# Cross-covariance attention with a highway layer: the loads' order, the start, and the place of one copy

## The chip, the cores and the metric

One core of a Trainium2 chip. The metric is the device time of one execution in microseconds (us); several executions of a kernel are timed and their median is compared. The engines are TensorE (PE, with its weight loads as PEld), VectorE (DVE), ScalarE (ACT), GpSimd (POOL) and SyncE (SP).

## What is computed

Inputs are float32: q, k, v of 4 batches x 6336 rows x 256 columns, two weights of 256x256, one bias. In short:

```python
qn = q / (norm(q, axis=1) + 1e-6);  kn = k / (norm(k, axis=1) + 1e-6)
a  = softmax(kn.transpose(0, 2, 1) @ qn / tau)      # 256 x 256 per batch
x  = (v @ a).reshape(25344, 256)
H  = maximum(x @ w_h, 0);  T = sigmoid(x @ w_t + b_t)
out = T * H + (1 - T) * x
```

## The kernel before

A batch is 49 tiles of 128 rows and a rest of 64 rows. **Phase 1** of a batch (`p1_tile`, L155) reads q and k and builds S = k'q and the diagonal blocks G of k'k and q'q in two PSUM banks, tile after tile. The **chain** (`chain`, L188) turns them into `mr`, a matrix of 256x768 that holds a, a·w_h and a·w_t: norms on DVE, a square root on POOL (`nrm`, L206), softmax on ACT and DVE, then products with the weights. **Phase 2** works in 25 slots per batch, 100 in all, each of two tiles of v. A slot multiplies the transposed v of its tiles with the three parts of `mr` (`mains`, L343, into `zbank`, `h`, `x`), and the same PE stream transposes v for the slot three ahead (`transpose`, L317, into the one PSUM buffer `vtps`), which `vt_copy` (L333) copies to SBUF as `vts`: on DVE for odd slots, on ACT for even ones. `elementwise_ops` (L374) makes the output: a sigmoid `tt` and a reseeding copy on ACT, `th` and `ux` on DVE, `o` on POOL, and a store by SP every four slots.

The program is written out by hand and each engine runs its instructions in that order. Phase 1 of batch 0 stands alone at the start; phase 1 of batch b+1 is spread over the slots of batch b by `P1_END` (batch 1 in slots 0 to 17, batch 2 in 18 to 42, batch 3 in 43 to 67), and its chain follows, a piece per slot.

POOL issues all loads. They are groups of 12, 12, 12, 9 and 4 tiles of q and k (`load_qk`, six buffers each) and of 16, 16 and 17 tiles of v (`load_v`, four buffers), cast to float16 on the way: 64 KB as it lands for each tile, half of what is read. The issues take eight completion semaphores in turn (DMASW0 to 7), so each waits for the load eight before it to have landed. In the kernel before, q and k of batch 0, the weights, v's first group and the first group of batch 1 are issued ahead of the constants (`ident`, from which the other engines' start hangs), and later groups in pairs when a buffer has come free.

Of the kernel before, what the change touches and what calls it, by code (L numbers as in the profile page):

```python
# [11 lines left out]
f32 = mybir.dt.float32  # L12
# [7 lines left out]
def kernel(  # L20
# [31 lines left out]
    NQG = len(QG)  # L52
    QRING = 6
    VG = [(0, 16), (16, 16), (32, 17)]
# [14 lines left out]
    def rows(src2d):  # L69
        return src2d[0:NF, :].rearrange("(p s) c -> p s c", s=NS)  # L70
# [1 line left out]

    q_t, k_t, qr_t, kr_t, v_t = {}, {}, {}, {}, {}

    def load_qk(n):
        b, g = divmod(n, NQG)
        if b >= B:
            return
        s0, ns = QG[g]
        q_t[n] = stream_pool.tile([P, 12, C], f16, tag="q_in", bufs=QRING, name=f"q{n}")  # L80
        k_t[n] = stream_pool.tile([P, 12, C], f16, tag="k_in", bufs=QRING, name=f"k{n}")
        nc.gpsimd.dma_start(out=q_t[n][:, 0:ns, :], in_=rows(q[b])[:, s0 : s0 + ns, :])  # L82
        nc.gpsimd.dma_start(out=k_t[n][:, 0:ns, :], in_=rows(k[b])[:, s0 : s0 + ns, :])
        if g == 0:
            qr_t[b] = stream_pool.tile([P, C], f16, tag="q_rem", bufs=2, name=f"qr{b}")
            kr_t[b] = stream_pool.tile([P, C], f16, tag="k_rem", bufs=2, name=f"kr{b}")
            nc.gpsimd.dma_start(out=qr_t[b][0:REM, :], in_=q[b][NF:N, :])
            nc.gpsimd.dma_start(out=kr_t[b][0:REM, :], in_=k[b][NF:N, :])

    def load_v(m):  # L90
        b, g = divmod(m, NVG)
        if b >= B:
            return
# [42 lines left out]
    btp = hx_tile("btp")  # L136
    nc.tensor.matmul(btp[:, 0, :], ones32[0:1, :], bt_sb, start=True, stop=True)  # L137
    btb = const_pool.tile([P, 2, C], f32, tag="btb")
    for u in range(2):
        nc.scalar.copy(out=btb[:, u, :], in_=btp[:, 0, :])  # L140
    zbank = []
    for i in range(2):
        zb = psum_pool.tile([P, 2, C], f32, tag=f"z{i}", name=f"zbank{i}")
        nc.tensor.matmul(
            zb[:, :, :], zeros[:, 0:P], zeros[:, :], start=True, stop=True,
            skip_group_check=True,
        )
        nc.scalar.copy(out=zb[:, :, :], in_=btb[:, :, :])
        zbank.append(zb)
# [27 lines left out]
    def group_ended(j):  # L177

        for g, (s0, ns) in enumerate(QG):
            if j == s0 + ns:  # L180
                return g
        return None
# [222 lines left out]
    loads_due = []  # L405
    for j in range(NS + 1):
        p1_tile(0, j)
        g = group_ended(j)
        if g is not None:
            load_qk(g + QRING)  # L410
    load_v(3)

    pend = chain(0)
    vps = {}
    for idx, (pe, rest) in enumerate(pend):
        if pe is not None:
            pe()
        rest()
        if idx < LOOK:
            vt_copy(idx, transpose(idx))  # L420


    total1 = (B - 1) * (NS + 1)
    done1 = 0
    chain_q = []

    def p1_target(t):
        lo = 0
        for i, e in enumerate(P1_END):
            if t < e:  # L430
                return i * (NS + 1) + (NS + 1) * (t + 1 - lo) // (e - lo)
            lo = e
        return total1

    for t in range(NSLOT):
        b, i = divmod(t, NPAIR)
        due, loads_due = loads_due, []
# [12 lines left out]
        elementwise_ops(t, z, h, x)  # L450
        if ps is not None:
            vt_copy(t + LOOK, ps)
            bb, ii = divmod(t + LOOK, NPAIR)
            for g, (s0, ns) in enumerate(VG):
                if 2 * ii + 2 == s0 + ns or (g == NVG - 1 and ii == NPAIR - 1):
                    loads_due.append((load_v, bb * NVG + g + VRING))
        for fn, arg in due:
            fn(arg)
# [45 lines left out]
```

## Time and profile before

| | us |
|---|---|
| median of 3 runs | 371.47 (371.08 to 371.8) |
| the profiled execution: its own time | 372.11 |
| its span in the trace | 369.9 |
| PE, DVE, ACT, POOL busy | 271.1, 178.2, 164.8, 170.6 |

Busy times are sums over stages with different limits. The sum of the prediction is made against the span; 2.2 us of the execution's own time lie around it, and that execution took 0.6 us more than the median.

### The profile page before, as it was taken

How to read it: one execution, taken by the hardware profiler on the slowest of the kernel's cores; microseconds unless marked ns; L12 is line 12 of the kernel's file. 1: busy time of each engine (PE TensorE's matmuls, PEld its weight loads, DVE VectorE, ACT ScalarE, POOL GpSimd, SP SyncE). 2: the span in 40 equal slices, each digit the busy share in tenths (PEclk: the TensorE clock that was granted, in tenths of full speed). 3: DMA queues.
4: the chain of work that ended last, by engine and by line, in shares of the span. 5: the costliest groups of instructions: out<-in, count | busy, mean ns of one | idle time of the engine just before them, and what ended most of it. 6: DMA issues, size and time to landing. Idle time of an engine off the chain costs nothing.

```text
span 369.9 us, 6923 instructions
## 1 busy us (share of the span) xinstructions
PE 271.1 (73%) x2844; PEld 226.2 (61%) x2844; DVE 178.2 (48%) x333; ACT 164.8 (45%) x286; POOL 170.6 (46%) x184
## 2 busy tenths in 40 slices
PE   0001996017999998889999978999999677777781
PEld 0000896014889887768888857788888454666660
DVE  0000001024555554775656566656656776667781
ACT  1000101013545446645554657455455856666660
POOL 5213112120464477445565653445455644555563
PEclk9999999555999999899999999999999989999997
DMA  7999999999149999999899993735629123222223
GB/s 133 213 214 212 213 216 214 211 214 217 20 143 215 261 265 264 240 226 240 214 204 295 199 223 119 114 136 153 191 113 223 39 93 135 116 113 116 113 115 135
DMA packets 13377, 65.58 MB, mean 177 GB/s; under 512 B 1569, under 2 KB 3618, under 8 KB 8738
## 3 DMA queue, kind: packets, MB, share of 16 engines
q0 software_dynamic: 8992, 39.19, 54.9%
q1 hardware_dynamic: 4354, 25.96, 17.2%
q8 instruction: 22, 0.36, 0.4%
q14 instruction: 9, 0.07, 0.1%
HBM read 78.38 MB, written 25.95 MB: 282 GB/s over the span
## 4 chain that ended last, share of the span: by engine, by line
PE 46%; DVE 19%; DMA 14%; issue 9%; POOL 6%; ACT 3%; DVEq 0%; POOLq 0%; ACTq 0%
DMA q<-in_q_dram 11%; PE h L347 10%; DVE ux L392 8%; PE S L169 8%; PE vtps L324 7%; PE zbank L347 6%; PE x L347 6%; DVE vts L339 6%; PE G L172 4%; PE G L175 4%; POOL o L398 3%; DVE th L387 3%; DMA k<-in_k_dram 3%; PE ah L273 1%; POOL nrm L206 1%
## 5 line engine op out<-in xcount | busy, mean ns | idle before, releaser
L398 POOL TENSOR_TENSOR o<-th,ux 128x512 f32<-128x512 f32 x96 | 123.8, 1291 | 127.4 <-DVE ux L392 106.0
L347 PEld LDWEIGHTS <-vts 128*128 128x128 f16 x1200 | 110.5, 99 | 17.5 <-issue 6.3
L387 DVE SCALAR_TENSOR_TENSOR th<-h,tt 128x512 f32<-128x512 f32 (+1 forms) x104 | 69.3, 669 | 83.9 <-PE h L347 55.3
L377 ACT ACTIVATE tt<-zbank 128x512 f32<-128x512 f32 x100 | 59.7, 597 | 90.3 <-PE zbank L347 89.4
L169 PE MATMUL S<-q,k 128*128 128x256 f16 x392 | 87.0, 276 | 0.0
L172 PE MATMUL G<-k 128*128 128x128 f16 x392 | 76.1, 221 | 0.0
L392 DVE SCALAR_TENSOR_TENSOR ux<-tt,x 128x512 f32<-128x512 f32 (+1 forms) x104 | 67.9, 656 | 0.1
L324 PE MATMUL vtps<-ident,v 128*128 128x128 f16 (+1 forms) x400 | 40.0, 222 | 30.9 <-DVE vts L339 27.8
L347 PE MATMUL zbank<-mr,vts 128*128 128x256 f16 (+1 forms) x400 | 61.5, 276 | 0.6 <-DVE mr L286 0.6
L347 PE MATMUL x<-mr,vts 128*128 128x256 f16 (+1 forms) x400 | 61.7, 277 | 0.0
L347 PE MATMUL h<-mr,vts 128*128 128x256 f16 (+1 forms) x400 | 61.4, 276 | 0.0
L379 ACT COPY zbank<-btb 128x512 f32<-128x512 f32 x98 | 57.8, 590 | 3.1
L324 PEld LDWEIGHTS <-v 128*128 128x128 f16 (+1 forms) x400 | 27.2, 99 | 45.9 <-DVE vts L339 37.6
L175 PE MATMUL G<-q 128*128 128x128 f16 x392 | 54.2, 220 | 0.0
L169 PEld LDWEIGHTS <-k 128*128 128x128 f16 x392 | 38.7, 99 | 4.1 <-issue 0.6
L339 ACT CAST vts<-vtps 128x512 f16<-128x512 f32 x48 | 27.9, 582 | 27.3 <-PE vtps L324 27.2
L172 PEld LDWEIGHTS <-k 128*128 128x128 f16 x392 | 38.8, 99 | 0.8
L339 DVE CAST vts<-vtps 128x512 f16<-128x512 f32 x48 | 32.8, 683 | 0.0
L175 PEld LDWEIGHTS <-q 128*128 128x128 f16 x392 | 30.4, 99 | 2.4
L137 PE MATMUL btp<-bt_sb,ones 1*128 1x256 f32 x2 | 1.2, 707 | 35.7 <-DVE ones L120 35.7
L82 POOL DMA_DIRECT2D q<-in_q_dram x20 | 11.4, 568 | 29.2 <-PE G L175 19.4
L137 PEld LDWEIGHTS btp<-bt_sb,ones 1*128 1x128 f32 x2 | 0.5, 308 | 35.7 <-DVE ones L120 35.7
(55 smaller groups left out, 108.3 us busy)
## 6 DMA issues: line engine op xcount, KB each, us to landing
out_dram<-o SPq DMA_DIRECT2D x24, 1024.0 KB, 4.6
q<-in_q_dram POOLq DMA_DIRECT2D x12, 768.0 KB, 13.2
k<-in_k_dram POOLq DMA_DIRECT2D x12, 768.0 KB, 17.8
v<-in_v_dram POOLq DMA_DIRECT2D x8, 1024.0 KB, 10.6
v<-in_v_dram POOLq DMA_DIRECT2D x4, 1088.0 KB, 14.7
q<-in_q_dram POOLq DMA_DIRECT2D x4, 576.0 KB, 17.9
k<-in_k_dram POOLq DMA_DIRECT2D x4, 576.0 KB, 18.6
q<-in_q_dram POOLq DMA_DIRECT2D x4, 256.0 KB, 15.7
```

The costliest lines, as they stand in the source:

```text
L82: nc.gpsimd.dma_start(out=q_t[n][:, 0:ns, :], in_=rows(q[b])[:, s0 : s0 + ns, :])
L169: nc.tensor.matmul(S[:, c, :], kc, qq[0:nr, :], start=first and c == 0, stop=last and c == 1)
L172: nc.tensor.matmul(G[:, c, :], kc, kc, start=first and c == 0, stop=False)
L175: nc.tensor.matmul(G[:, 2 + c, :], qc, qc, start=False, stop=last and c == 1)
L324: nc.tensor.matmul(ps[:, u, c, 0 : nr[u]], vt[0 : nr[u], s + u, bass.ts(c, P)], ident[0 : nr[u], 0 : nr[u]], start=(u == 0 and c == 0), st ...
L339: cp(out=sb, in_=ps)
L347: nc.tensor.matmul(dst[0:r, u, :], sb[:, u, kt, 0:r], mr[:, kt, off : off + C], start=(not seeded and kt == 0 and (u == 0 or i == NPAIR - 1)),
L377: nc.scalar.activation(out=tt, in_=z, func=Act.Sigmoid)
L379: nc.scalar.copy(out=z, in_=btb)
L387: nc.vector.scalar_tensor_tensor(out=th[pr, us, :], in0=h[pr, us, :], scalar=0.0, in1=tt[pr, us, :], op0=AluOp.max, op1=AluOp.mult,)
L392: nc.vector.scalar_tensor_tensor(out=ux[pr, us, :], in0=tt[pr, us, :], scalar=1.0, in1=x[pr, us, :], op0=AluOp.subtract, op1=AluOp.mult,)
L398: nc.gpsimd.tensor_tensor(out=ot[pr, o0 + us.start : o0 + us.stop, :], in0=th[pr, us, :], in1=ux[pr, us, :], op=AluOp.subtract,)
```

## The change

The weights, constants and loads of the start change places; the loads of q and k are separate, sorted by the slot that needs them, and issued one per slot (three at a time at two places of the start); the groups of q and k of batches 1 to 3 run 4, 9, 12, 12, 12 tiles, and the rest of 64 rows is worked last in place of first; four tiles of batch 1's phase 1 (`HEAD`) go into the chain of batch 0, and the seeding of `zbank` from the bias (`btp`, `btb`) behind phase 1 of batch 0; the copy `vts` goes ahead of `th` and `ux`; a chain's PE piece stands behind the slot's products and its other piece behind the elementwise work.

```diff
-    QG = [(0, 12), (12, 12), (24, 12), (36, 9), (45, 4)]
+    QG = [spans(12, 12, 12, 9, 4)] + [spans(4, 9, 12, 12, 12)] * (B - 1)
+    HEAD = 4
...
-    for n in range(NQG):
-        load_qk(n)
-    wht = const_pool.tile([P, 2, 2 * C], f16, tag="wht")
...
-    load_v(0)
-    load_qk(NQG)
+    load_q(0)
+    load_k(0)
     bt_sb = const_pool.tile([1, C], f32, tag="bt")
...
     nc.vector.memset(zeros.bitcast(u16), 0)
-    load_v(1)
-    load_v(2)
+    for n in range(1, NQG):
+        load_q(n)
+        load_k(n)
+    load_qr(0)
+    load_kr(0)
+    wht = const_pool.tile([P, 2, 2 * C], f16, tag="wht")
...
+    load_q(NQG)
+    load_k(NQG)
+    load_v(0)
...
-        if j == 0:
+        if j == NS:
             kk, qq, nr = kr_t[b], qr_t[b], REM
...
-    def elementwise_ops(t, z, h, x):
+    def elementwise_ops(t, z, h, x, ps):
         nc.scalar.activation(out=tt, in_=z, func=Act.Sigmoid)
+        if ps is not None:
+            vt_copy(t + LOOK, ps)
...
+    want.sort()
+    def next_loads(k):
+        while k and want:
+            _, _, fn, arg, dep = want[0]
+            if dep is not None and dep not in ready:
+                return
+            want.pop(0)
+            fn(arg)
+            k -= 1
...
     for j in range(NS + 1):
         p1_tile(0, j)
-        if g is not None:
-            load_qk(g + QRING)
-    load_v(3)
+    ready = set(used)
+    next_loads(3)
+    btp = hx_tile("btp")
+    nc.tensor.matmul(btp[:, 0, :], ones32[0:1, :], bt_sb, start=True, stop=True)
...
+        if idx == 5:
+            next_loads(3)
+        if idx == 2:
+            while done1 < HEAD:
+                p1_tile(1, done1)
...
         mains(t, z, 2 * C, True)
         ps = transpose(t + LOOK) if t + LOOK < NSLOT else None
-        if pe_part is not None:
-            pe_part()
         mains(t, h, C, False)
         mains(t, x, 0, False)
-        if rest_part is not None:
-            rest_part()
-        elementwise_ops(t, z, h, x)
-        if ps is not None:
-            vt_copy(t + LOOK, ps)
+        if pe_part is not None:
+            pe_part()
+        elementwise_ops(t, z, h, x, ps)
+        if rest_part is not None:
+            rest_part()
+        next_loads(1)
```

POOL at the start. Before, the constant `ident` stands behind 19 loads; here the last of them (names carry the buffer's number):

```order
L96 DMA v_96<-in_v_dram 128x4096 [waits DMASW6_49]
L82 DMA q_98<-in_q_dram 128x3072 [waits DMASW7_49]
L83 DMA k_99<-in_k_dram 128x3072 [waits DMASW0_49]
L87 DMA qr_102<-in_q_dram 64x256 [waits DMASW1_49]
L88 DMA kr_103<-in_k_dram 64x256 [waits DMASW2_49]
masks.py:197 MEMSET ident_108 128x128
```

With the change the same place is reached after two loads that wait for nothing:

```order
L88 DMA q_69<-in_q_dram 128x3072
L94 DMA k_71<-in_k_dram 128x3072
masks.py:197 MEMSET ident_75 128x128
masks.py:199 ISA
masks.py:199 AFFINE_SELECT ident_75<-ident_75 128x128 [waits Pool_49]
L88 DMA q_90<-in_q_dram 128x3072
```

`ident` has moved ahead of all loads that wait for another to land. Next, POOL from the end of batch 0's phase 1, before:

```order
L82 DMA q_457<-in_q_dram 128x3072 [waits DMASW6_49,PE_49]
L83 DMA k_458<-in_k_dram 128x3072 [waits DMASW7_49]
L87 DMA qr_461<-in_q_dram 64x256 [waits DMASW0_49]
L88 DMA kr_462<-in_k_dram 64x256 [waits DMASW1_49]
L96 DMA v_465<-in_v_dram 128x4096 [waits DMASW2_49]
L206 TENSOR_TENSOR nrm_482<-n_0_468,half 128x4 [waits DVE_49]
```

and with the change, on into the first slots:

```order
L88 DMA q_425<-in_q_dram 128x3072 [waits DMASW3_49,PE_49]
L205 TENSOR_TENSOR nrm_446<-n_0_439,half 128x4 [waits DVE_49]
L206 TENSOR_TENSOR nrm_446<-nrm_446,eps 128x4 [waits Pool_49]
L94 DMA k_493<-in_k_dram 128x3072 [waits DMASW4_49]
L108 DMA v_495<-in_v_dram 128x4096 [waits DMASW5_49]
L88 DMA q_497<-in_q_dram 128x3072 [waits DMASW6_49,PE_49]
L399 TENSOR_TENSOR o_563<-th_559,ux_560 128x512 [waits DVE_49]
L94 DMA k_565<-in_k_dram 128x3072 [waits DMASW7_49]
L399 TENSOR_TENSOR o_563<-th_603,ux_604 128x512 [waits DVE_49]
L88 DMA q_608<-in_q_dram 128x3072 [waits DMASW0_49,PE_49]
```

16 loads stood between those 19 and `nrm`, 35 in all; now 20 stand ahead of it, and from slot 0 each `o` but a few is followed by one load with a wait of its own. Last, DVE in slots 0 to 2, before:

```order
L387 SCALAR_TENSOR_TENSOR th_554<-h_541,tt_551 128x512
L392 SCALAR_TENSOR_TENSOR ux_555<-tt_551,x_546 128x512
L339 CAST vts_560<-vtps_536 128x512
L387 SCALAR_TENSOR_TENSOR th_598<-h_585,tt_595 128x512
L392 SCALAR_TENSOR_TENSOR ux_599<-tt_595,x_590 128x512
```

and with the change:

```order
L338 CAST vts_556<-vtps_539 128x512
L388 SCALAR_TENSOR_TENSOR th_559<-h_544,tt_554 128x512
L393 SCALAR_TENSOR_TENSOR ux_560<-tt_554,x_549 128x512
L388 SCALAR_TENSOR_TENSOR th_603<-h_588,tt_598 128x512
L393 SCALAR_TENSOR_TENSOR ux_604<-tt_598,x_593 128x512
```

The copy stands ahead of the `th` and `ux` of its slot. PE's order within a slot (zbank, vtps, h, x, q/k tiles) is the same in both.

## Rows read from the trace of the kernel before

**Rows 1.** The page: span, granted TensorE clock and DMA share in 40 slices
```profile
span 369.9 us, 6923 instructions
...
PEclk9999999555999999899999999999999989999997
DMA  7999999999149999999899993735629123222223
```

**Rows 2.** Timeline, POOL, 0 to 37: start, us, engine line op, [idle before <-releaser]
```profile
8.77 0.54 POOL L82 DMA_DIRECT2D q<-in_q_dram  x1 [3.06 <-DMA q<-in_q_dram]
12.40 0.53 POOL L83 DMA_DIRECT2D k<-in_k_dram  x1 [3.10 <-DMA k<-in_k_dram]
...
32.94 0.52 POOL L87 DMA_DIRECT2D qr<-in_q_dram  x1 [2.19 <-DMA k<-in_k_dram]
...
35.49 1.20 POOL L96 DMA_DIRECT2D v<-in_v_dram  x2 [0.20 <-issue]
```

**Rows 3.** Timeline, PE, its first instruction
```profile
35.74 1.22 PE L137 MATMUL btp<-bt_sb,ones 1*128 1x256 f32 x2 [35.74 <-DVE ones L120]
```

**Rows 4.** Timeline, POOL, the last load ahead of batch 0's chain
```profile
77.22 0.56 POOL L96 DMA_DIRECT2D v<-in_v_dram  x1 [2.29 <-DMA q<-in_q_dram]
77.81 1.06 POOL L206 TENSOR_TENSOR nrm<-n,half 128x4 f32<-128x4 f32 x1
```

**Rows 5.** Timeline, ACT: the sigmoids of slots 0, 18, 43, 68, 75, 99
```profile
90.22 0.60 ACT L377 ACTIVATE tt<-zbank 128x512 f32<-128x512 f32 x1
...
141.29 0.60 ACT L377 ACTIVATE tt<-zbank 128x512 f32<-128x512 f32 x1
...
213.99 0.60 ACT L377 ACTIVATE tt<-zbank 128x512 f32<-128x512 f32 x1
...
286.76 0.60 ACT L377 ACTIVATE tt<-zbank 128x512 f32<-128x512 f32 x1
...
308.55 0.60 ACT L377 ACTIVATE tt<-zbank 128x512 f32<-128x512 f32 x1 [0.70 <-DVE ux L392]
...
360.37 0.60 ACT L377 ACTIVATE tt<-zbank 128x512 f32<-128x512 f32 x1 [1.02 <-PE zbank L347]
```

**Rows 6.** Timeline, PE, slots 29 and 30 (with q/k tiles)
```profile
176.04 0.60 PE L347 MATMUL zbank<-mr,vts 128*128 128x256 f16 x4
176.96 0.40 PE L324 MATMUL vtps<-ident,v 128*128 128x128 f16 x4 [0.32 <-DVE vts L339]
...
178.95 0.60 PE L347 MATMUL zbank<-mr,vts 128*128 128x256 f16 x4
...
181.37 0.49 PE L347 MATMUL zbank<-mr,vts 128*128 128x256 f16 x3
```

**Rows 7.** Timeline, PE, slots 84 and 85 (no q/k tiles left)
```profile
328.41 0.60 PE L347 MATMUL zbank<-mr,vts 128*128 128x256 f16 x4
...
329.94 0.60 PE L347 MATMUL zbank<-mr,vts 128*128 128x256 f16 x4
...
332.86 0.60 PE L347 MATMUL zbank<-mr,vts 128*128 128x256 f16 x4
```

**Rows 8.** Waits, whole span: engine line <- releaser: us, times, longest
```profile
PE vtps L324 <- DVE vts L339: 27.8, 37, 2.3
```

**Rows 9.** The page's groups on DVE: shapes, count, busy us, mean ns, idle before
```profile
L387 DVE SCALAR_TENSOR_TENSOR th<-h,tt 128x512 f32<-128x512 f32 (+1 forms) x104 | 69.3, 669 | 83.9 <-PE h L347 55.3
...
L392 DVE SCALAR_TENSOR_TENSOR ux<-tt,x 128x512 f32<-128x512 f32 (+1 forms) x104 | 67.9, 656 | 0.1
...
L339 DVE CAST vts<-vtps 128x512 f16<-128x512 f32 x48 | 32.8, 683 | 0.0
```

**Rows 10.** The page's DMA queues: packets, MB, share of 16 engines
```profile
q0 software_dynamic: 8992, 39.19, 54.9%
q1 hardware_dynamic: 4354, 25.96, 17.2%
```

**Rows 11.** Windows: start:end us, busy by engine, clock, DMA share, GB/s
```profile
120.00:136.00 16.00, 16.00 (x191) 14.40 (x188) 8.83 (x15) 7.96 (x14) 10.45 (x12) 1.00 1.04 271
```

More of the change, by code (lines that the diff above doesn't have):

```diff
@@ L50, with spans @@
     NF = NS * P
-    QG = [(0, 12), (12, 12), (24, 12), (36, 9), (45, 4)]
-    NQG = len(QG)
+    def spans(*sizes):
+        got, s0 = [], 0
+        for ns in sizes:
+            got.append((s0, ns))
+            s0 += ns
+        assert s0 == NS
+        return got
+    QG = [spans(12, 12, 12, 9, 4)] + [spans(4, 9, 12, 12, 12)] * (B - 1)
+    NQG = 5
     QRING = 6
-    VG = [(0, 16), (16, 16), (32, 17)]
+    VG = spans(16, 16, 17)
     NVG = len(VG)
@@ L73, with load_q, load_k, load_qr @@
     q_t, k_t, qr_t, kr_t, v_t = {}, {}, {}, {}, {}
-    def load_qk(n):
+    def load_q(n):
         b, g = divmod(n, NQG)
-        if b >= B:
-            return
-        s0, ns = QG[g]
+        s0, ns = QG[b][g]
         q_t[n] = stream_pool.tile([P, 12, C], f16, tag="q_in", bufs=QRING, name=f"q{n}")
+        nc.gpsimd.dma_start(out=q_t[n][:, 0:ns, :], in_=rows(q[b])[:, s0 : s0 + ns, :])
+    def load_k(n):
+        b, g = divmod(n, NQG)
+        s0, ns = QG[b][g]
         k_t[n] = stream_pool.tile([P, 12, C], f16, tag="k_in", bufs=QRING, name=f"k{n}")
-        nc.gpsimd.dma_start(out=q_t[n][:, 0:ns, :], in_=rows(q[b])[:, s0 : s0 + ns, :])
         nc.gpsimd.dma_start(out=k_t[n][:, 0:ns, :], in_=rows(k[b])[:, s0 : s0 + ns, :])
[L84 to L88, printed above, removed]
+    def load_qr(b):
+        qr_t[b] = stream_pool.tile([P, C], f16, tag="q_rem", bufs=2, name=f"qr{b}")
+        nc.gpsimd.dma_start(out=qr_t[b][0:REM, :], in_=q[b][NF:N, :])
+    def load_kr(b):
+        kr_t[b] = stream_pool.tile([P, C], f16, tag="k_rem", bufs=2, name=f"kr{b}")
+        nc.gpsimd.dma_start(out=kr_t[b][0:REM, :], in_=k[b][NF:N, :])
     def load_v(m):
         b, g = divmod(m, NVG)
-        if b >= B:
-            return
         s0, ns = VG[g]
@@ L126 @@
     nc.vector.memset(zeros.bitcast(u16), 0)
-    load_v(1)
-    load_v(2)
+    for n in range(1, NQG):
[4 more added lines that the diff above has]
+    wht = const_pool.tile([P, 2, 2 * C], f16, tag="wht")
+    nc.gpsimd.dma_start(
+        out=wht[:, :, 0:C], in_=moe_w_h.rearrange("(kt jl) m -> jl kt m", kt=2)
+    )
+    nc.gpsimd.dma_start(
+        out=wht[:, :, C : 2 * C], in_=moe_w_t.rearrange("(kt jl) m -> jl kt m", kt=2)
+    )
+    load_q(NQG)
+    load_k(NQG)
+    load_v(0)
     def hx_tile(name):
         return psum_pool.tile([P, 2, C], f32, tag="hx", bufs=3, name=name)
[L136 to L149, printed above, removed]
     S_t, G_t = {}, {}
+    used = set()
     def p1_tile(b, j):
@@ L158, in p1_tile @@
             G_t[b] = psum_pool.tile([P, 4, P], f32, tag="G", name=f"G{b}")
+        if j == NS:
             kk, qq, nr = kr_t[b], qr_t[b], REM
         else:
-            s = j - 1
-            g = max(i for i in range(NQG) if QG[i][0] <= s)
+            g = max(i for i in range(NQG) if QG[b][i][0] <= j)
             n = b * NQG + g
-            kk, qq, nr = k_t[n][:, s - QG[g][0], :], q_t[n][:, s - QG[g][0], :], P
+            o = j - QG[b][g][0]
+            kk, qq, nr = k_t[n][:, o, :], q_t[n][:, o, :], P
         S, G = S_t[b], G_t[b]
@@ L175, in p1_tile @@
             nc.tensor.matmul(G[:, 2 + c, :], qc, qc, start=False, stop=last and c == 1)
[L177 to L182, printed above, removed]
+        for g, (s0, ns) in enumerate(QG[b]):
+            if j == s0 + ns - 1:
+                used.add(("q", b * NQG + g))
     mr_t = {}
@@ L402, in elementwise_ops, with p1_target, p1_slot @@
         store(t, ot)
-    loads_due = []
+    total1 = (B - 1) * (NS + 1)
+    def p1_target(t):
+        lo, base = 0, HEAD
+        for i, e in enumerate(P1_END):
+            if t < e:
+                return base + ((i + 1) * (NS + 1) - base) * (t + 1 - lo) // (e - lo)
+            lo, base = e, (i + 1) * (NS + 1)
+        return total1
+    def p1_slot(n):
+        return next(t for t in range(-1, NSLOT) if p1_target(t) > n)
+    want = []
+    for n in range(NQG + 1, B * NQG):
+        b, g = divmod(n, NQG)
+        at = p1_slot((b - 1) * (NS + 1) + QG[b][g][0])
+        dep = ("q", n - QRING)
+        want.append((at, len(want), load_q, n, dep))
+        want.append((at, len(want), load_k, n, dep))
@@ new lines @@
+    for b in range(1, B):
+        at = p1_slot((b - 1) * (NS + 1) + NS)
+        want.append((at - 1, len(want), load_qr, b, None))
+        want.append((at - 1, len(want), load_kr, b, None))
+    for m in range(1, B * NVG):
+        b, g = divmod(m, NVG)
+        at = b * NPAIR + VG[g][0] // 2 - LOOK
+        want.append((at, len(want), load_v, m, ("v", m - VRING) if m >= VRING else None))
+        if g == NVG - 1:
+            want.append((at, len(want), load_vr, b, None))
+    want.sort()
[7 more added lines that the diff above has]
+            k -= 1
@@ L406 @@
     for j in range(NS + 1):
         p1_tile(0, j)
-        g = group_ended(j)
-        if g is not None:
-            load_qk(g + QRING)
-    load_v(3)
-    pend = chain(0)
-    vps = {}
-    for idx, (pe, rest) in enumerate(pend):
+    ready = set(used)
+    next_loads(3)
+    btp = hx_tile("btp")
+    nc.tensor.matmul(btp[:, 0, :], ones32[0:1, :], bt_sb, start=True, stop=True)
+    btb = const_pool.tile([P, 2, C], f32, tag="btb")
+    for u in range(2):
+        nc.scalar.copy(out=btb[:, u, :], in_=btp[:, 0, :])
@@ L416 @@
+    zbank = []
+    for i in range(2):
+        zb = psum_pool.tile([P, 2, C], f32, tag=f"z{i}", name=f"zbank{i}")
+        nc.tensor.matmul(
+            zb[:, :, :], zeros[:, 0:P], zeros[:, :], start=True, stop=True,
+            skip_group_check=True,
+        )
+        nc.scalar.copy(out=zb[:, :, :], in_=btb[:, :, :])
+        zbank.append(zb)
+    done1 = 0
+    pieces = chain(0)
+    for idx, (pe, rest) in enumerate(pieces):
+        if idx == 5:
+            next_loads(3)
         if pe is not None:
@@ L418 @@
         rest()
[L419 to L424, printed above, removed]
-    chain_q = []
[L427 to L433, printed above, removed]
+        if idx == 2:
+            while done1 < HEAD:
+                p1_tile(1, done1)
+                done1 += 1
+        if idx == 5:
+            vt_copy(0, transpose(0))
+    for t in range(1, LOOK):
+        vt_copy(t, transpose(t))
+    chain_q = []
     for t in range(NSLOT):
         b, i = divmod(t, NPAIR)
-        due, loads_due = loads_due, []
+        ready = set(used)
         pe_part, rest_part = chain_q.pop(0) if chain_q else (None, None)
@@ L455 @@
                 if 2 * ii + 2 == s0 + ns or (g == NVG - 1 and ii == NPAIR - 1):
[L456 to L458 removed]
+                    used.add(("v", bb * NVG + g))
         while done1 < p1_target(t):
```

13 lines of the change are left out of this document (2 added, 11 removed).

## The prediction

> **What bounds the kernel now.** I read the page's slices first, then the timelines of POOL and PE at the start, then PE in two clean slots, then the waits, and the DMA queues last.
>
> The span is 369.9 us, and the DMA engines are full for its first tenths while PE does little [rows 1]. PE's first instruction starts at 35.74, released by a constant on DVE [rows 3]. That constant hangs on `ident`, which POOL makes behind 19 loads. POOL issues eight loads at once and then one whenever the load eight before it has landed: q's first group at 8.77, k's at 12.40, k's fourth at 32.94, k's fifth by 35.49 [rows 2]. So PE begins when the last group of batch 0 is already there. The same thing happens a second time: POOL is held by loads until 77.22, and only then makes `nrm`, at 77.81, on which the chain of batch 0 waits [rows 4]. The first sigmoid starts at 90.22 [rows 5].
>
> From there PE sets the pace. In slot 30 it goes from `zbank` to `zbank` in 2.42 us (178.95 to 181.37); slot 29 took 2.91, since its transposes waited for `vts` on DVE [rows 6]. Without q and k tiles slot 84 takes 1.53 us, and slot 85, with that wait, 2.92 [rows 7]. So one q/k tile costs (2.42 - 1.53) / 2 = 0.445 us, and the wait costs 0.49 us per two slots in the first case, 1.39 in the second. The waits view counts 27.8 us of it in 37 pieces [rows 8], less than these gaps, since PE's modelled ends reach into them.
>
> **The start.** The loads of batch 0 keep their total, so they land by about 35.4 as before. What moves is the work on them. With `ident` behind two loads, PE can start when k's first group has landed, at 12.40, and then follows the loads: a group of 12 needs 12 x 0.445 = 5.3 us and lands every 7.3 (two loads of 3.63, 8.77 to 12.40 [rows 2]). The fourth group lands 0.3 us ahead of 32.94, since the two small rest loads now come later; the 9 + 4 tiles left take 5.8 us and the rest tile some 0.5: 38.9. At the lower clock that PE shows in the slices after its long wait ("5", half [rows 1]), tiles cost twice as much and the end is 6 us later; I take the full clock, as PE has work in most of each interval, and keep the 6 us for the range. The norms on DVE take 1.3 us, my allowance: four instructions that together read as many columns as one `vts` copy, 683 ns [rows 9], taken twice. POOL's loads ahead of `nrm` are then 20, and the last of them waits for the rest of batch 0, so POOL is free by 37 and `nrm` waits for DVE alone. From `nrm` to the first sigmoid it was 90.22 - 77.81 = 12.4 us [rows 4, 5]. The third transpose now has to wait for the second's copy before slot 0: 0.68 [rows 9] and some 0.4 for the transposes, 1.1. The four `HEAD` tiles lie beside the softmax and the bias products beside the norms: nothing; if softmax were ready sooner, they would cost 1.8. First sigmoid: 38.9 + 1.3 + 12.4 + 1.1 = **53.7** in place of 90.22.
>
> **The slots.** Slots 0 to 17 took 141.29 - 90.22 = 51.07 us [rows 5]. Four of 50 tiles are gone (4 x 0.445 = 1.8). With three tiles in most slots little is left of the wait for `vts`; between nothing and nine times 0.49 I take 1.0: **48.3**.
>
> Slots 18 to 42 took 72.70 us and 43 to 67 took 72.77 [rows 5]. With the copy ahead of `th` it starts when the transposes are done and ends before PE's next transposes: 11 of the 12 or 13 waits per batch go, 11 x 0.49 = 5.4. The chain costs what it did: its products no longer hold up `h` and `x`, but the next batch's first tile needs the S and G banks, and they are now read behind `th` and `ux`. **67.3 and 67.4.**
>
> Slots 68 to 74 hold the last chain: 308.55 - 286.76 = 21.79, of which three waits of 1.39 could go; I take half, 2.1: **19.7**. Slots 75 to 98 took 360.37 - 308.55 = 51.82. PE alone would need 24 x 1.53 = 36.7. DVE has `th`, `ux` and half a copy per slot, 669 + 656 + 342 = 1.67 us of durations [rows 9], 40.0 in all, though it starts one within less than the length of the one before. Between the two I take 1.60 a slot: **38.4**, a gain of 13.4. The tail behind the last sigmoid stays at 369.9 - 360.37 = **9.5**.
>
> **What the loads do.** The stage of slots 18 to 30 is where the new order can hold the kernel. One load per slot is more than the DMA can land, so the queue fills, and then POOL stands at a load while `o` waits behind it. `th` and `ux` have three buffers, so DVE can run two slots ahead of POOL and PE a little more. The load of slot 27 needs the one of slot 19 (v's sixth group) landed. By then the queue has carried q and k of batches 0 to 2 without a rest, six groups of v and the weights: 18,944 + 6,304 + 256 = 25,504 KB, beside six stores. Between 12.40 and 32.94 it landed 4,288 KB, 209 KB a us [rows 2], so 122 us. A store of 1,024 KB takes 2.57 us by the store queue's share (17.2% of 369.9 us for 25,344 KB [rows 10]). With 5.1 us ahead of the first bytes (8.77 less 3.67) that is 5.1 + 122 + 15.4 = 142.5. By the sum above, POOL would be there at about 130 (sigmoid 27 at 53.7 + 48.3 + 24.2 = 126.2, and 3.2 for `th`, `ux`, `o`). Two slots of slack and `th` of slot 31 as the first that must wait leave 2 to 6 us; I take **4**. By the load queue's share of the whole span (54.9% for 38,272 KB, 188 KB a us [rows 10]) it would land at 156 and hold the kernel by some 16. The stretch 120 to 136 is nearer to the first: 271 GB/s in 16 us is 4,234 KB, of which 5.6 slots' stores are 1,434 KB and 3.6 us, so loads ran at 226 [rows 11].
>
> **Sum.** 53.7 + 48.3 + 67.3 + 67.4 + 19.7 + 38.4 + 9.5 + 4 = 308.3 us of span. With the 2.2 us around the span and less the 0.6 by which the profiled execution lay above the median: **310 us** against 371.47.
>
> **Rivals.** (a) The loads set the pace into slot 30: the hold is 16 in place of 4, and slots 0 to 17 lose 4 us waiting for v's third group (it lands at some 86 to 89 by the rate of 209, and slot 13 needs it at 53.7 + 13 x 2.68 = 88.5): 326. For it: the DMA share stays at 9 in most slices of the first half, with less asked of it per us [rows 1]; against: rows 11.
> (b) The copy's place gives nothing: `th` starts later by one copy, `x` of the next slot needs `th`'s PSUM buffer, and PE waits there. All gains of that part go: 1.0 + 5.4 + 5.4 + 2.1 + 13.4 = 27.3, so 337. For it: DVE has 1.67 us of durations against 1.53 on PE; against: with q/k tiles a slot is 2.42, and `th` there has room.
> (c) Slower: PE follows landings, in short bursts, and the clock falls to half in all slots that share with loads, 0 to 42. Each slot then costs 2.42 more: 43 x 2.42 = 104, so 414. It decides from 26 slots on (61.5 / 2.42). For it: where PE waits for batch 0's chain, three slices show 5 [rows 1]. Against: PE has 1.5 to 2.4 us of work per slot and no hold here is near 15 us. The Trainium skill (TensorE: Matmul & The Clock Gate, "Loop structure matters more than you think") warns of just this, a DMA wait between bursts of matmuls that sends the clock down; in the slots of this trace the rows show it at 9.
>
> (d) The loads run a fifth slower all through, 173 KB a us: batch 0 lands 6 us later and the hold grows from 4 to 29, 341. For it: the 188 of rows 10 is half-way there; against: 209 over 20 us in rows 2, which is 1.573 MB of float32 read in 3.63 us, 433 GB/s. The Trainium skill (SBUF — State Buffer, "Summary: rules for kernel authors") says to estimate transfers from HBM at about 358 GB/s, which is such a rate; in the first 35 us this trace disagrees with it.
>
> **How the numbers follow.** About 0.2% is what a measurement can tell from no change here. Forecast 0.70, (a) 0.16, (b) 0.08, (c) 0.03, (d) 0.02, and 0.01 for no change, which none of these mechanisms gives. Below, the hold goes (4), slots 0 to 17 lose all nine waits (3.4), the last stage is PE's (1.7), the chain gives its other half (2.1): 310 - 11.2, 298.8. Above, (a) at 326, or a cold start (6) with the last stage half-way (1.85 a slot, another 6): 322. I give **298 to 328**; (b), (c) and (d) lie outside, with 0.13. Faster 0.96, same 0.01, slower 0.03.
>
> **What would show it.** Right: PE's first product of q and k near 12.4, `nrm` near 40, the first sigmoid near 54; slots of 2.42 in pairs without a wait, last slots near 1.6; the wait of `vtps` for `vts` nearly gone; POOL waiting for DMA in slots 11 and 20 to 28 for up to 13 us, and DVE's `th` for POOL for a few. Wrong: sigmoid 0 later than 62; POOL's waits for DMA passing whole into `th`; last slots above 1.9; a granted clock of half anywhere past the start.

## The result and the profile after

The changed kernel takes **318.83 us** (316.53 to 320.99 over four runs); the kernel before took 371.35 (371.08 to 371.8) beside it. The ratio is 0.858, with a 95% interval of 0.852 to 0.865. The forecast was 310.0, with a range of 298 to 328: sign and range held, and the size was 9 us too good. The profiled execution has a span of 318.9 us; it was the longest of the four, 2.2 above their median, so its stages add up to 10.6 us more than the forecast's span of 308.3. An execution more than 1.5% above the fastest of its kernel is left out of the ratios; below this is one execution of a_near.

First PE's slices in the kernel before, then the page of the kernel after, against [rows 1]: its span and three of its rows of slices.

```profile
PE   0001996017999998889999978999999677777781
```

```profile
span 318.9 us, 6923 instructions
...
PE   0597977999998698997999687999999586999990
...
PEclk9997979999999979999999979999999876899996
DMA  6999999999999999999999999947449303034534
```

PE now works from the second slice on, where before it stood until the fifth. Three dips are left, each with a drop of the clock beside it: these are the three chains in the slots. Now the stages, by the sigmoids of slots 0, 18, 43, 68, 75 and 99 as in [rows 5], and of slots 25 and 50 (timeline of ACT: start and length in us, then line, operation, and in brackets the idle time before it and who ended it):

```profile
53.30 0.60 ACT L376 ACTIVATE tt<-zbank 128x512 f32<-128x512 f32 x1
...
100.96 0.60 ACT L376 ACTIVATE tt<-zbank 128x512 f32<-128x512 f32 x1 [1.50 <-PE zbank L346]
...
128.03 0.60 ACT L376 ACTIVATE tt<-zbank 128x512 f32<-128x512 f32 x1 [1.17 <-PE zbank L346]
...
173.59 0.60 ACT L376 ACTIVATE tt<-zbank 128x512 f32<-128x512 f32 x1 [1.41 <-PE zbank L346]
...
202.18 0.60 ACT L376 ACTIVATE tt<-zbank 128x512 f32<-128x512 f32 x1 [1.17 <-PE zbank L346]
...
245.89 0.60 ACT L376 ACTIVATE tt<-zbank 128x512 f32<-128x512 f32 x1 [1.06 <-PE zbank L346]
...
271.99 0.60 ACT L376 ACTIVATE tt<-zbank 128x512 f32<-128x512 f32 x1 [2.68 <-PE zbank L346]
...
309.32 0.60 ACT L376 ACTIVATE tt<-zbank 128x512 f32<-128x512 f32 x1 [0.88 <-PE zbank L346]
```

The differences, beside the forecast's terms. A chain's pieces lie in slots 18 to 24, 43 to 49 and 68 to 74, so the stages that begin with a chain are cut once more, at the sigmoids of slots 25 and 50 (166.13 and 238.62 in the kernel before).

| stage | before | forecast | after |
|---|---|---|---|
| start, to the first sigmoid | 90.22 | 53.7 | 53.30 |
| slots 0 to 17 | 51.07 | 48.3 | 47.66 |
| slots 18 to 42 with the hold | 72.70 | 71.3 | 72.63 |
| of it the chain's slots 18 to 24 | 24.84 | | 27.07 |
| slots 43 to 67 | 72.77 | 67.4 | 72.30 |
| of it the chain's slots 43 to 49 | 24.63 | | 28.59 |
| slots 68 to 74 (chain) | 21.79 | 19.7 | 26.10 |
| slots 75 to 98 | 51.82 | 38.4 | 37.33 |
| tail | 9.5 | 9.5 | 9.6 |

Outside the chains the forecast stands: slots 50 to 67 take 43.71 us, 2.43 each, and most of the last ones 1.53 or 1.54. All three chains grew, where they should have kept their cost or lost some of it. The waits of the kernel after that bear on this (engine and line, what it waited for: us in total, times, longest):

```profile
PE cq L219 <- DVE dcat L211: 10.4, 4, 3.4
PE at L257 <- DVE mr L247: 4.1, 3, 1.5
DVE inv L208 <- POOL nrm L206: 10.2, 4, 3.4
DVE th L388 <- POOL o L399: 6.3, 3, 4.3
PE vtps L323 <- DVE vts L338: 1.2, 1, 1.2
```

The wait of the transposes for `vts`, 27.8 us in [rows 8], is down to 1.2; small steps of the chain stand in its place. `cq`, the chain's first product, waits for `dcat` on DVE, and that for the square root `nrm` on POOL.

### The profile page after: what moved, and what is told of

It is laid out like the page before. It is cut to its first block, busy times and chain, and to the rows that moved or that the text cites. A ratio compares the mean times of both kernels' runs of the same rounds, so it can differ in the third digit from the quotient of the medians.

```text
span 318.9 us, 6923 instructions
## 1 busy us (share of the span) xinstructions
PE 271.5 (85%) x2844; PEld 234.1 (73%) x2844; DVE 178.1 (56%) x333; ACT 157.1 (49%) x286; POOL 169.7 (53%) x184
## 4 chain that ended last, share of the span: by engine, by line
PE 44%; DMA 34%; POOL 7%; DVE 6%; ACT 4%; issue 2%; POOLq 0%; DVEq 0%
DMA v<-in_v_dram 18%; DMA q<-in_q_dram 9%; PE zbank L346 8%; PE h L346 8%; PE x L346 7%; PE S L171 7%; DMA k<-in_k_dram 7%; PE vtps L323 4%; POOL o L399 4%; PE G L174 4%; PE G L177 4%; DVE ux L393 2%; POOL nrm L205 1%; PE ah L272 1%; DVE th L388 1%
## 5 line engine op out<-in xcount | busy, mean ns | idle before, releaser
L171 PE MATMUL S<-q,k 128*128 128x256 f16 x392 | 90.9, 285 | 15.5 <-DMA k<-in_k_dram 13.7
L174 PE MATMUL G<-k 128*128 128x128 f16 x392 | 79.2, 227 | 1.5 <-DVE junk L195 1.5
L346 PE MATMUL zbank<-mr,vts 128*128 128x256 f16 (+1 forms) x400 | 62.7, 279 | 0.6 <-DVE mr L285 0.6
L380 ACT COPY zbank<-btb 128x512 f32<-128x512 f32 x98 | 58.7, 599 | 1.6
L177 PE MATMUL G<-q 128*128 128x128 f16 x392 | 56.1, 227 | 0.0
L171 PEld LDWEIGHTS <-k 128*128 128x128 f16 x392 | 40.1, 102 | 19.8 <-DMA k<-in_k_dram 13.8
L174 PEld LDWEIGHTS <-k 128*128 128x128 f16 x392 | 40.1, 102 | 3.6 <-issue 2.4
L323 PEld LDWEIGHTS <-v 128*128 128x128 f16 (+1 forms) x400 | 31.0, 99 | 7.8 <-issue 4.2
L177 PEld LDWEIGHTS <-q 128*128 128x128 f16 x392 | 31.8, 102 | 3.0
L338 ACT CAST vts<-vtps 128x512 f16<-128x512 f32 x48 | 27.8, 580 | 3.8 <-PE vtps L323 3.8
L195 DVE SCALAR_TENSOR_TENSOR junk<-G,ident 128x128 f32<-128x128 f32 x16 | 3.7, 286 | 36.5 <-PE G L177 36.5
```

The source lines that it names most:

```text
L171: nc.tensor.matmul(S[:, c, :], kc, qq[0:nr, :], start=first and c == 0, stop=last and c == 1)
L323: nc.tensor.matmul(ps[:, u, c, 0 : nr[u]], vt[0 : nr[u], s + u, bass.ts(c, P)], ident[0 : nr[u], 0 : nr[u]], start=(u == 0 and c == 0), st ...
L338: cp(out=sb, in_=ps)
L346: nc.tensor.matmul(dst[0:r, u, :], sb[:, u, kt, 0:r], mr[:, kt, off : off + C], start=(not seeded and kt == 0 and (u == 0 or i == NPAIR - 1)),
```

## The experiments

Each was timed beside the kernel before. The labels with b_ are the kernel before with one part of the change in it, those with a_ the kernel after with one edit, and those with c_ carry several edits.

**b_ident: constants behind four loads in place of nineteen.**

```diff
-    for n in range(NQG):
-        load_qk(n)
+    load_qk(0)
...
     nc.vector.memset(zeros.bitcast(u16), 0)
+    for n in range(1, NQG):
+        load_qk(n)
...
     load_v(1)
```

> The kernel before with the constants issued behind the first four loads in place of behind nineteen; the other loads keep their order and stay ahead of the chain's root on POOL. Theory: PE starts near 12 us, but the root stays behind 35 loads and so near 77: 370 to 372. Rival: PE's late start is itself the loss, phase 1 ends 22 us sooner and so does everything: 345 to 352.

Measured: 372.18, ratio 1.000 [0.9986, 1.0021]. PE started early and then stood at `nrm`, which POOL still made behind the later loads; the first sigmoid came at 90.64. Nothing, as expected: the second hold stands right behind the first.

**b_nrm: the 13 loads that were issued behind phase 1 and ahead of `nrm` put behind it.**

```diff
         p1_tile(0, j)
-        g = group_ended(j)
-        if g is not None:
-            load_qk(g + QRING)
-    load_v(3)
...
         rest()
+        if idx == 1:
+            for g in range(NQG):
+                load_qk(g + QRING)
+            load_v(3)
```

> The kernel before with the 13 loads that follow phase 1 moved behind the chain's root; the constants stay late. Theory: the root runs when phase 1 ends, near 62.5 in place of 77.8; the 13 loads then stand ahead of the first o until the fifth of them has landed, near 83, so slot 3 is at 84 in place of 98.7: 355 to 359. Rival: the queue of loads sets the pace and the root's time is nothing: 369 to 372.

Measured: 366.36, ratio 0.985 [0.983, 0.988], less than expected. The first sigmoid did come at 74.94, 15.3 us earlier. Slots 0 to 17 gave 2.1 of it back (53.13 against 51.07), and the chain's slots 18 to 24 another 7.0 (31.87 against 24.84): its root stood on POOL behind loads that waited for landings.

```profile
133.85 0.53 POOL L83 DMA_DIRECT2D k<-in_k_dram  x1 [1.82 <-DMA k<-in_k_dram]
138.97 0.52 POOL L87 DMA_DIRECT2D qr<-in_q_dram  x1 [4.60 <-DMA v<-in_v_dram]
...
140.02 1.05 POOL L206 TENSOR_TENSOR nrm<-n,half 128x4 f32<-128x4 f32 x1
```

**b_start: the two diffs above together.**

> Both of the former: constants early and the 13 loads behind the root. Theory: the root runs near 40.5 and the first sigmoid near 53, but the 13 loads stand ahead of the first o until the queue has landed all of v's first two groups, batch 1's first group and two more, near 78; DVE runs three slots and stands: 350 to 354, a gain of 17 to 21. Rival (the start's term of the sum, 36.5 us, needs no interleaving of loads and slots): 333 to 337.

Measured: 357.0, ratio 0.960 [0.958, 0.962], above its range. The first sigmoid came at 53.86, 36.4 us earlier, as in the kernel after; 21.3 of that was given back, 15.2 in slots 0 to 17 (66.30 against 51.07) and 6.1 in the first chain (30.94 against 24.84). The timelines of POOL and of DVE show where:

```profile
74.75 0.51 POOL L88 DMA_DIRECT2D kr<-in_k_dram  x1 [3.15 <-DMA k<-in_k_dram]
77.53 0.57 POOL L96 DMA_DIRECT2D v<-in_v_dram  x1 [2.27 <-DMA q<-in_q_dram]
```

```profile
79.43 0.69 DVE L388 SCALAR_TENSOR_TENSOR th<-h,tt 128x512 f32<-128x512 f32 x1 [17.30 <-POOL o L399]
```

A load on POOL waits until the one eight before it has landed, and `o` stood behind the loads; it began at 78.12. So the start alone is not worth what it moves; it needs loads that are spread out, which is the change's other half.

**b_copy: only the copy of transposed v put ahead of `th` and `ux`.**

```diff
         nc.scalar.activation(out=tt, in_=z, func=Act.Sigmoid)
+        if ps is not None:
+            vt_copy(t + LOOK, ps)
...
-        elementwise_ops(t, z, h, x)
+        elementwise_ops(t, z, h, x, ps)
         if ps is not None:
-            vt_copy(t + LOOK, ps)
```

> The kernel before with the copy of transposed v ahead of th and ux, nothing else. Forecast: 27.3 us less than 371.4, so 342 to 347. Rival: the copy delays th and x as much as it speeds the transposes: 369 to 373.

Measured: 341.08, ratio 0.918 [0.915, 0.920]: 30.7 us, somewhat more than the 27.3 of the prediction.

**a_copy_back: the reverse, the copy behind `th` and `ux` in the kernel after.**

```diff
         nc.scalar.activation(out=tt, in_=z, func=Act.Sigmoid)
-        if ps is not None:
-            vt_copy(t + LOOK, ps)
...
             rest_part()
+        if ps is not None:
+            vt_copy(t + LOOK, ps)
```

> The changed kernel with the copy of transposed v back behind th and ux. Forecast: the term of the prediction, 27.3 us, comes back: 344 to 348. Rival: in the changed kernel the loads hold the pace up to slot 32, so the copy is worth only the later stages (5.4 + 2.1 + 13.4): 338 to 341. Second rival, the copy's place gives nothing: 319.

Measured: 348.87, ratio 0.941 [0.937, 0.945], 30.0 above the kernel after. The two agree, so the copy's place is worth 30 us with either order of loads. Slots 75 to 98 take 51.09 again in place of 37.33: 13.8 for that stage, where the prediction had 13.4. Rival (b), that the place gives nothing, falls.

**a_chain_old: in the kernel after, both pieces of each chain back ahead of the slot's work.**

```diff
     ps = transpose(t + LOOK) if t + LOOK < NSLOT else None
+    if pe_part is not None: pe_part()
...
     mains(t, x, 0, False)
-    if pe_part is not None: pe_part()
+    if rest_part is not None: rest_part()
     elementwise_ops(t, z, h, x, ps)
-    if rest_part is not None: rest_part()
```

> The changed kernel with both halves of a chain's pieces back where they stood (the PE piece ahead of h and x, the other half ahead of the elementwise work). Theory: their new places cost the changed kernel 10.5 us (its chains' seven slots take 27.1, 28.6 and 26.1 us, those of the kernel before 24.8, 24.6 and 21.8), so 319 - 10 = 307 to 311. Rival: the chains got slower by the fuller DMA queue or by the copy's new place, and the pieces' places do nothing: 317 to 321.

Measured: 310.7, ratio 0.836 [0.832, 0.839]. The chains' slots take 21.82, 24.54 and 19.45 us where the kernel after has 27.07, 28.59 and 26.10: 16.0 less in all. The sigmoids of slots 18, 25, 43, 50, 68 and 75:

```profile
102.77 0.60 ACT L376 ACTIVATE tt<-zbank 128x512 f32<-128x512 f32 x1
...
124.59 0.60 ACT L376 ACTIVATE tt<-zbank 128x512 f32<-128x512 f32 x1 [1.37 <-PE zbank L346]
...
174.72 0.60 ACT L376 ACTIVATE tt<-zbank 128x512 f32<-128x512 f32 x1
...
199.26 0.60 ACT L376 ACTIVATE tt<-zbank 128x512 f32<-128x512 f32 x1 [1.01 <-PE zbank L346]
...
242.97 0.60 ACT L376 ACTIVATE tt<-zbank 128x512 f32<-128x512 f32 x1
...
262.42 0.60 ACT L376 ACTIVATE tt<-zbank 128x512 f32<-128x512 f32 x1 [0.48 <-PE zbank L346]
```

The timeline of ACT shows the last chain of this kernel, around its softmax (`tt` is a slot's sigmoid, `ar` the chain's exponential, which needs another table):

```profile
246.03 0.60 ACT L376 ACTIVATE tt<-zbank 128x512 f32<-128x512 f32 x1
...
247.27 1.28 ACT L235 ACT_TABLE_LOAD   x1
250.35 0.51 ACT L235 ACTIVATE ar<-t,inv 128x256 f32<-128x256 f32 x1 [1.80 <-DVE t L224]
...
251.46 1.28 ACT L376 ACT_TABLE_LOAD   x1
252.75 0.60 ACT L376 ACTIVATE tt<-zbank 128x512 f32<-128x512 f32 x1
```

The same stretch of the kernel after:

```profile
249.00 0.62 ACT L376 ACTIVATE tt<-zbank 128x512 f32<-128x512 f32 x1
...
255.61 0.60 ACT L376 ACTIVATE tt<-zbank 128x512 f32<-128x512 f32 x1 [5.37 <-PE zbank L346]
...
257.15 1.28 ACT L235 ACT_TABLE_LOAD   x1
258.44 0.51 ACT L235 ACTIVATE ar<-t,inv 128x256 f32<-128x256 f32 x1
...
259.55 1.28 ACT L376 ACT_TABLE_LOAD   x1
260.85 0.60 ACT L376 ACTIVATE tt<-zbank 128x512 f32<-128x512 f32 x1
```

With the pieces ahead, the wait for `cq`, both table loads and the exponential lie in one gap between two sigmoids, 6.7 us. With the pieces behind, a sigmoid gets in between them: first 6.6 us in which the slot's products stand behind `cq`, then 5.2 in which its successor's sigmoid stands behind table loads and exponential. The chain's end repeats this: slots 73 and 74 take 3.5 and 6.5 us in the kernel after, 5.1 and 1.7 in this one. The two earlier chains lose time at their beginning as well: slots 18 and 43 take 4.41 and 4.35 us in the kernel after, 2.41 and 2.42 here. There the next batch's first tile waits on PE for the copy of S (`ssb` on ACT) and the norms that read G (`junk` on DVE), which now stand behind the slot's elementwise work; that is 4 of the 16 us.

Yet only 8 us of the 16 reach the time (10 between the two profiled executions). Slots 25 to 42 take 50.13 us in place of 45.56: the first chain ends 3.4 us sooner, at 124.59 against 128.03, and slot 43 begins at 174.72 against 173.59. DVE's timeline says why; `th` now waits 10.9 us for `o`, which stands on POOL behind loads:

```profile
136.91 0.69 DVE L388 SCALAR_TENSOR_TENSOR th<-h,tt 128x512 f32<-128x512 f32 x1 [2.96 <-POOL o L399]
...
146.16 0.69 DVE L388 SCALAR_TENSOR_TENSOR th<-h,tt 128x512 f32<-128x512 f32 x1 [4.00 <-POOL o L399]
```

Slots 0 to 17 hold no chain, and the edit doesn't touch them; that they take 51.40 us in place of 47.66 is a matter of slot 13, told under c_old_near_root.

**a_rest_old: only the pieces on DVE, ACT and POOL back ahead; PE's stay behind.**

```diff
     if pe_part is not None: pe_part()
+    if rest_part is not None: rest_part()
     elementwise_ops(t, z, h, x, ps)
-    if rest_part is not None: rest_part()
```

> The changed kernel with only the non-PE half of a piece back ahead of the elementwise work; PE pieces stay behind the products. Theory: the longest waits of the chains are PE's at cq for dcat (2.1, 2.9, 3.4 us), because the root on POOL stands behind o; with the half ahead these 8.4 us go, though th and ux wait for the root instead: 309 to 314. Rival as above: 317 to 321. A second rival, that th and ux waiting for the root cost as much as cq's wait: no gain here but one in the split kernel.

Measured: 314.34, ratio 0.847 [0.842, 0.852]; chains of 23.32, 23.28 and 21.88. These pieces make 13.3 of the lost 16 us (81.8 less 68.5); the exponential and the table loads are among them. Slot 43 begins at 175.32, so much of it is eaten again. The other 2.7 us are PE's places.

**a_split: kernel after, with the norms and the square root in the chain's first slot, ahead of that slot's elementwise work and `o`.**

```diff
-            (None, norms),
+            (None, both(norms, roots)),
...
+        if rest_part is not None and t == first_piece:
+            rest_part()
         elementwise_ops(t, z, h, x, ps)
-        if rest_part is not None:
+        if rest_part is not None and t != first_piece:
             rest_part()
```

(`roots` are the two POOL lines with `nrm` cut out of `invs`; `first_piece` is the slot of a chain's first piece.)

> The changed kernel with the norms and the root on POOL together in a chain's first slot, ahead of its elementwise work; all other pieces as in the changed kernel. Theory: cq's wait for dcat (8.4 us in three chains) and the first tile's wait for S and G (3.2 us) go, and nothing is held for them: 307 to 311. Rival (the chains' cost is the exponential's table loads and the softmax's length, not the root): 315 to 320.

Measured: 315.83, ratio 0.850 [0.845, 0.854]: the rival's numbers. The chains take 22.98, 28.03 and 22.95. Two of three lose 3 to 4 us, so the rival's reason doesn't hold, only its time. The second loses almost nothing: there `nrm` came at 179.61, behind a load that stood on POOL for 4.07 us. And slot 43 begins at 173.50 as before. A chain that ends sooner gains nothing while POOL stands at a load.

So the next runs ask whether it is the transfers that set slot 43's start near 174, or only the order in which POOL issues them.

**a_near: kernel after, a load at most 14 slots ahead of its need.**

```diff
-    if dep is not None and dep not in ready:
+    if at > now + 14 or dep is not None and dep not in ready:
         return
```

(In `next_loads`; `at` is the slot that needs the load, `now` the one being issued.)

> The kernel after, with one edit: a load is issued at most 14 slots ahead of the slot that needs it, so that fewer loads stand on POOL's queue ahead of o. Theory (a load stands on POOL only because it was issued earlier than a landing allows, and o behind it holds th): the 6.3 us for which th waits for o in the kernel after fall below 3, slots 18 to 42 take some 2 us less than 72.6, the time is 316 to 318 against 318.8. Rival (the transfers themselves set the time at which slot 43 can begin, at 173.5 to 175.3 us in every kernel with this order of loads so far): slot 43 begins at 173 or later, the wait moves to the products of q and k or to the transposes of v, and the time is 318 to 321.

Measured: 317.51 (315.17 to 320.43), ratio 0.852 [0.847, 0.857]. Slots 25 to 42 fall from 45.56 to 43.71, which is 2.43 a slot, as in slots 50 to 67 of the kernel after; `th` waits 1.5 us for `o` in place of 6.3, and slot 43 begins at 171.27. The hold was 1.85 us here, and it goes. The time alone can't tell this from the kernel after, as the two intervals overlap. The chains take 26.66, 27.43 and 25.33, 79.4 in all.

**c_old_near: the diffs of a_chain_old and a_near together.**

> The kernel after with the chain's and the tiles' products back behind the slot's own, and loads issued at most 14 slots ahead. Theory: the two or three slots around 13 and 31 to 33 in which th waits 9 to 11 us for o because POOL stands at a load lose most of that; slot 43 begins near 169 in place of 174.7, and the time is 303 to 306 against 310.7 without the bound on loads. Rival (the transfers set slot 43's start): slot 43 begins at 173 to 175 again, with the wait on PE in place of DVE, and the time is 309 to 312.

Measured: 302.05, ratio 0.812 [0.810, 0.814], 8.7 under a_chain_old and better than the range given. (The expectations of this run and the next two have some of the places the wrong way round, and no edit moves the q/k tiles; the diffs are as told here: pieces ahead.) ACT's sigmoids of slots 25 and 43, which came at 124.59 and 174.72 in a_chain_old:

```profile
124.86 0.60 ACT L376 ACTIVATE tt<-zbank 128x512 f32<-128x512 f32 x1 [1.36 <-PE zbank L346]
...
168.57 0.60 ACT L376 ACTIVATE tt<-zbank 128x512 f32<-128x512 f32 x1
```

From the same point, 43.71 us in place of 50.13, with the same bytes. So it was not the transfers: the rival falls. Loads that nobody needed yet stood on POOL ahead of `o`. The chains take 64.3 here and 79.4 in a_near, 15.1 apart: the pieces' places cost the same without such a hold.

**c_old_near_root: c_old_near, with the root in the chain's first slot.**

```diff
-            (None, norms),
+            (None, both(norms, roots)),
```

> As the kernel with both parts of the chain behind the slot's products and loads at most 14 slots ahead, and the square root of the norms is issued on POOL in the chain's first slot, ahead of that slot's o, in place of the second. Theory (the chain's length is set by what its small steps queue behind): one slot's o less ahead of the root, so 0 to 1.3 us per chain, 0 to 4 us in all: 299 to 306. Rival (the root waits for the norms on DVE and holds up o instead): same time or up to 2 us more.

Measured: **297.0** (296.86 to 297.53), ratio 0.799 [0.798, 0.801], 5 us less and 2 under the range. The chains take 21.27, 21.04 and 17.79, which is 4.2 less in all, so 0.6 to 2.0 each; slots 0 to 17 lose 2.5 more (48.83 against 51.35), which no edit here touches. It is slot 13, which takes 4.2 us in place of 6.7: its transposes wait for v's third group. PE's timeline of c_old_near, then of this run:

```profile
87.51 0.43 PE L323 MATMUL vtps<-ident,v 128*128 128x128 f16 x4 [2.46 <-DMA v<-in_v_dram]
```

```profile
87.08 0.40 PE L326 MATMUL vtps<-ident,v 128*128 128x128 f16 x4 [1.60 <-DMA v<-in_v_dram]
```

The group lands at nearly the same time in all eight kernels with this order of loads and the copy ahead (these transposes start at 87.07 to 87.51), whether the first sigmoid came at 51.4 or, as in the profiled execution of the kernel after, at 53.3. Behind the wait the granted clock from 88.3 to 92 us was 0.61 in c_old_near and 1.00 here. From these transposes to the next slot's `zbank` it was 3.63 us there (to 91.14) and 1.99 here (to 89.07), so some 1.6 of the 2.5 us are clock, and none are the root's. The page of this run:

```profile
span 294.8 us, 6917 instructions
...
PE   0397977999979998999999999999999969999980
...
PEclk9999998999999999999999999999999999999995
```

Of the three dips that the kernel after shows in PE's slices, the first is an 8 and the second is gone, and the clock holds through all the chains. This version beats both kernels, by 20.1% and some 6.8% (297.0 against 318.83).

**c_rest_near_root: the same with PE's pieces left behind `x`, so the diffs of a_rest_old, a_near and the root's.**

> As the kernel after, with only the chain's steps on DVE, ACT and POOL back behind the slot's element-wise work (PE's products of the chain stay ahead of h and x), loads at most 14 slots ahead, and the root in the chain's first slot. Theory (the non-PE steps are what lengthened the chain): chains of 22 to 23 us, last one 20 to 22, time 301 to 307, within 2 us of the same kernel with PE's products moved as well. Rival (PE's place matters too): 3 us or more above that kernel.

Measured: 301.33, ratio 0.812 [0.809, 0.814], 4.3 above: the rival's side of the line, so PE's place matters too. The chains take 21.89, 21.66 and 20.16, which is 3.6 of it.

## Why the prediction came out as it did

**The start held.** PE's first product of q and k came at 11.70 (12.40 forecast), `nrm` at 41.33 (40.2), the first sigmoid at 53.30 (53.7). Two small errors cancel in the last of these: `nrm` came 1.1 us late, and from there it was 12.0 us in place of 13.5. Rows of PE and POOL:

```profile
11.70 0.40 PE L171 MATMUL S<-q,k 128*128 128x256 f16 x1 [11.70 <-DMA k<-in_k_dram]
```

```profile
41.33 1.04 POOL L205 TENSOR_TENSOR nrm<-n,half 128x4 f32<-128x4 f32 x1 [4.36 <-DVE junk L195]
```

`nrm` waits for DVE alone, not for a load, as the prediction had it.

**The copy held**, and was a little undersized: 27.3 forecast, 30.0 and 30.7 by two runs. The last stage came out at 37.33 / 24 = 1.56 us a slot, near PE's own 1.53 of [rows 7], where 1.60 was taken. The lengths of DVE's instructions, 1.67 a slot by [rows 9], did not bind it.

**The hold of POOL held in place, and was 1.85 us where 4 was taken.** The load that was forecast to land at 142.5 released POOL at 144.61, and `th` waited for `o` there:

```profile
144.61 0.57 POOL L108 DMA_DIRECT2D v<-in_v_dram  x1 [4.08 <-DMA v<-in_v_dram]
```

```profile
146.52 0.69 DVE L388 SCALAR_TENSOR_TENSOR th<-h,tt 128x512 f32<-128x512 f32 x1 [4.30 <-POOL o L399]
```

It was small only because the chain before it took longer: a_chain_old, without those 5 us, held for 6.4 (50.13 less 43.71). The working had a slip here too: it reached sigmoid 27 at 126.2 by spreading 67.3 us evenly over 25 slots, where its own chain of 23.7 in the first seven makes 130.5; it came at 132.86. POOL waited for landings in slots 11, 26 and 27, for 2.5, 2.7 and 4.1 us.

**The step that failed is "The chain costs what it did".** With 18 slots of 2.42 taken from the forecast's 67.3 and 67.4, it left 23.7 and 23.8 us for the two chains with q/k tiles, and 19.7 for the last one, 67.2 in all. The kernel after takes 81.8. That is 14.6 over; the hold (2.0 less), the last stage (1.1), slots 0 to 17 (0.6) and the start (0.4) came out under, and 308.3 + 14.6 - 4.1 = 318.8, within 0.1 of the span. a_chain_old shows this cause: with only the chain's places undone, the chains take 65.8. So with the old places the term would have held. The argument looked at what the chain holds up (`h` and `x`) and not at what holds up the chain; it did name the first tile's wait for S and G, and gave it nothing, where it took 4 us. A piece behind the slot's work begins a slot's products or elementwise work later, and each piece waits for the one before it on another engine. That the time still fell into the range is luck as far as the chains go: the range was held open upwards for late loads, a cold start and a slower last stage, and had the chain only on its lower side.

Part of it is the clock. Windows of the kernel after, around the last chain (us, busy time and count of PE, PEld, DVE, ACT and POOL, granted clock, DMA share, GB/s):

```profile
249.00:254.00 5.00, 1.56 (x12) 1.16 (x10) 2.31 (x7) 1.20 (x3) 2.83 (x4) 0.83 0.38 157
254.00:258.00 4.00, 4.00 (x20) 2.53 (x19) 2.60 (x5) 2.37 (x5) 1.29 (x1) 0.50 0.19 72
258.00:264.00 6.00, 3.75 (x32) 2.88 (x29) 3.72 (x6) 5.49 (x11) 2.43 (x2) 0.91 0.00 0
264.00:272.00 8.00, 6.39 (x31) 2.68 (x32) 5.03 (x11) 1.78 (x4) 2.82 (x4) 0.62 0.40 156
```

After 3.44 us at `cq` PE runs at 0.50, the lower level (1.2 GHz), for 4 us without a pause, so 2 us of that stretch are the clock's; it is low again at 264 to 272, after the wait for `mr`. Over the last chain's slots the mean clock is 0.75 and PE's busy time 18.80 us, against 0.91 and 15.53 in a_chain_old. This is the sign "a granted clock of half anywhere past the start", which the prediction had named for being wrong. The Trainium skill (TensorE: Matmul & The Clock Gate, "Loop structure matters more than you think") tells of a DMA wait that sends the clock down; here a wait for DVE came before it.

**The other rivals.** (a) and (d), with the loads setting the pace, would have shown in slots 25 to 42: these are within 1.85 us of the 43.71 that a_near takes there. The load that (d) would have made 25 us later landed 2.1 us behind its forecast. Of (a) one part came: v's third group landed near 87, as it said. In the kernel after PE waited 0.4 us for it, in those with an earlier first sigmoid 1.6 to 2.5, so a still earlier start would gain nothing unless that group lands sooner (not tried). (c), the lower clock in all slots that share with loads, did not come: those slots took 2.43 at the full clock. Among the slots the clock fell in and right behind the chains alone, which no rival had; it fell in two slices of the start as well (7 in the page above).

What can't be told apart is how much of the gain is the order of loads by itself: b_copy and b_start give 30.7 and 14.8, a_chain_old, with the chains where they were, 61.0 (371.66 less 310.7). The other 15.5 us come from the order of the loads, from what it lets the early start keep, and from the parts that no run took alone (`HEAD`, the sizes of the groups, the rest worked last); the three sums need not add up.

## What to carry to other kernels

In this kernel a chain of small dependent steps on several engines belongs ahead of the wide work of its slot: ask of a moved step what it now waits behind, not only what it sets free. A load that is issued from a queue with compute on it costs when it is issued too early, since it stands there until an older one has landed; bound how far ahead it may go. And fix them together: the faster chain was worth 8 us with early loads and the bound some 1 us with the slow chain (not clear of the noise), but both together 17.

## What the runs showed of the hardware

- DVE's pair of scaled casts that makes `mr` takes 0.62 us at the start, where no `o` runs, and 1.65 to 1.67 in each chain in the slots, where POOL's `o` begins with it (at 262.84 in the last one). The pair of `dcat` shows the same: 0.48 in the kernel after, 1.25 to 1.49 in c_old_near_root, where an `o` begins up to 0.3 us ahead of it. Wide float32 steps on DVE that read a PSUM operand (`th`, `ux`, `vts`) took 0.67 to 0.69 beside an `o`. Three times 1.05 us on the chain's path; moving `o` away from it was not tried.

```profile
46.30 0.62 DVE L247 TENSOR_SCALAR mr<-ar,rinv 128x256 f16<-128x256 f32 x2
...
262.88 1.67 DVE L247 TENSOR_SCALAR mr<-ar,rinv 128x256 f16<-128x256 f32 x2
```

- A wait of 3.4 us on PE was followed by 4 us at half the clock in the kernel after; in c_old_near_root, whose waits for `cq` are 2.0 us at most, the clock stays at 9 in the slices of all three chains.
